# An attention and mixture-of-experts kernel: first-weight splits and block transposes placed along the second products, evictions in program order

## The chip, the cores and the metric

The kernel runs on one core of a Trainium2 chip. The metric is the device time of one execution in microseconds (us). Lower is better. The engines that matter here: TensorE (PE, matrix products; its weight loads are shown as PEld), ScalarE (ACT), VectorE (DVE), GpSimd (POOL, which here mostly issues gathers and scatters) and SyncE (SP, which issues the loads).

## The reference

Attention over 8 batches of 448 tokens with 12 heads of 64, with a soft cap on the scores, then a mixture of 8 experts of which each token goes to one. The second half is what the change touches:

```
scores = cap * tanh(q @ k.T * scale / cap);  attn = softmax(scores) @ v
x      = attn, 3584 tokens of 768
logits = x @ w_gate + modality_bias[modality_id];  e_idx = argmax(logits)
for e in range(8):
    mask = e_idx == e
    h = relu(x[mask] @ w1[e])              # 768 -> 1024
    out[mask] = gate_w[mask] * (h @ w2[e]) # 1024 -> 768
```

## The kernel before, in words

*Blocks.* After the attention the tokens are sorted by expert and done in blocks. In the profiled execution there are eight full blocks of 384 tokens (three tiles of 128), then two blocks of 256 (two tiles), then a rest of at most 32 tokens. Each block has its own expert, or a part of one, and loads that expert's weights.

*Precision.* Every operand of a product is split into a high part (rounded to fp32r) and a low part (what is left), and each product is done three times: high by high, high by low, low by high. Splitting a chunk of weights (`split_w`, lines 952 to 958) is a cast on ACT (line 954) and a subtraction on DVE (line 955). First weights (w1) have six chunks of 128 x 1024, their parts are named ah and al; second weights (w2) have eight chunks of 128 x 768, named bh and bl.

*One block* (`run_slot`, line 1066) runs as follows.
- `load_w2` (line 966) loads and splits the second weights of this block. These are not pinned.
- `ahead` (line 1182) has GpSimd compute an index tile (`index`, line 894) and gather the rows of the next block into `xg` (`gather`, line 928).
- `ffn1` (line 1006) does the first products, lines 1021 to 1025: 8 groups of 18 matmuls, each group into one of three PSUM buffers. ACT evicts a group with a relu (line 1031, hh) and DVE takes the low part (line 1032, hl), after which the buffer is free.
- `load_w1` (line 960) loads and splits the first weights of the next block, and behind its chunks 1 and 3 calls `transpose_all` (line 989): three block transposes of the gathered rows on DVE (line 993), three casts on ACT (line 1002) and three subtractions on DVE (line 1004) for the next block's x.
- `ffn2` (line 1037) does the second products, line 1055: for each tile two halves of 384 columns, 24 matmuls each. In the first tile the halves are interleaved: 21 products of the first half, 9 of the second, the last 3 of the first, and then the rest of the second. A half goes into one of two PSUM buffers (py); when it is done ACT scales it into `ot` (line 1060), and GpSimd scatters the tile to the output (line 1061).

*What sets the order.* Each engine works through one queue in order. The order is laid down before the run by a scheduler that follows program order and estimated readiness, except that an instruction wrapped in `pin` (line 93) stays behind the instruction of its engine that was written before it. `load_w1`, `split_x` within `transpose_all` and the loads are pinned; the eviction of line 1060 is not. Because `load_w1` is written ahead of `ffn2`, all of its instructions have their place in program order ahead of every eviction of `ffn2`.

*Raw buffers.* Loads go to four raw buffers (`load_raw`, line 945) shared by both kinds of weights, in the order first weights of the next block, second weights of the next block, and so on; SP issues a load when the chunk four earlier has been subtracted.

*The last blocks.* The first block of all (`between`) and the rest of few tokens take other ways through `run_slot`; for the blocks of two tiles `load_w2` is written behind `ffn1`.

Of the kernel before, what the change touches and what calls it, by code (L numbers as in the profile page):

```python
# [39 lines left out]
F32 = mybir.dt.float32  # L40
F32R = mybir.dt.float32r
BF16 = mybir.dt.bfloat16
I32 = mybir.dt.int32
# [6 lines left out]
B, H, S, D = 8, 12, 448, 64  # L50
# [11 lines left out]
TW = W // 128  # L62
# [3 lines left out]
KC, FC = DM // 128, FF // 128  # L66
HALF = DM // 2
# [16 lines left out]
class Program:  # L84
# [8 lines left out]
    def pin(self, inst):  # L93
        return self.tc.keep_in_program_order(inst)
# [798 lines left out]

    def index(self, raw, blocks, name="at"):

        at = self.ip.tile([128, 4 * TW], I32, name=name, bufs=2 if name == "at" else 1)
        for t, n in blocks:
            n, w = max(n, 1), 4 * max(n, 1)
            to = at[:, 4 * t : 4 * t + w].rearrange("p (t g) -> p g t", g=4)
            src = raw.bitcast(I32)[:, 4 * t : 4 * t + w, 0].rearrange("p (g t) -> p g t", g=4)  # L900
            self.pin(self.nc.gpsimd.tensor_scalar(to, src, 4.0, self.quarter, op0=ALU.mult, op1=ALU.add))
        return at

    def rows_few(self, meta, row):

        nc = self.nc
        r = self.register(nc.gpsimd, meta[row : row + 1, 1:2], NOROW)
        mt = self.lp.tile([128, 2], F32, name="mf")
        for g in range(4):
            self.pin(nc.gpsimd.dma_start(mt[g * FEW : (g + 1) * FEW], self.mapd[ds(r, FEW)]))  # L910
        index = self.lp.tile([128, 1], I32, name="index")
        self.pin(nc.gpsimd.tensor_scalar(
            index, mt.bitcast(I32)[:, 0:1], 4.0, self.quarter, op0=ALU.mult, op1=ALU.add
        ))
        return mt, index
# [41 lines left out]
            self.pin(a)  # L957
            self.pin(b)

    def load_w1(self, e, spread=True, n=0):  # L960
        for k in range(KC):
            self.split_w(self.load_raw(e, self.w1, k, FF, spread), self.w1s[k], pin=True)
            if n and k in (1, 3):
                self.transpose_all(n, range(3) if k == 1 else range(3, KC))

    def load_w2(self, e, raws=(), ks=range(FC)):
        for k in ks:
# [18 lines left out]
            if pin or t == 0:  # L986
                self.pin(move)

    def transpose_all(self, n, ks=range(KC)):
        turned = [self.lp.tile([128, S], F32, name="turned", tag="xT", bufs=4)[:, : n * 128] for _ in range(3)]  # L990
        for first in ks[::3]:
            for k, out in zip(range(first, first + 3), turned):
                self.pin(self.nc.vector.transpose(
                    out.rearrange("p (c x) -> p c x", x=32),
                    self.xg.bitcast(F32)[:, : 4 * n].rearrange("p c (x k) -> p k c x", k=KC)[:, k],
                ))
            self.split_x(range(first, first + 3), turned, n, pin=self.pin)

    def split_x(self, ks, pts, n=TW, pin=lambda inst: inst):
        w = n * 128  # L1000
# [33 lines left out]
                if at == f:  # L1034
                    work()

    def ffn2(self, mt, n, at={}):

        nc = self.nc
        for t in range(n):  # L1040
            ot = self.lp.tile([128, C * 256], F32, name="ot", tag="late", bufs=3)[:, :DM]
            rows = slice(t * 128, (t + 1) * 128)
            steps = [[(half, f, a, c) for f in range(FC) for a, c in ((0, 0), (0, 1), (1, 0))] for half in range(2)]
            if t == 0:
                late = [(0, f, 0, 1) for f in range(FC - 3, FC)]
                steps = [[step for step in steps[0] if step not in late] + steps[1][:9] + late, steps[1][9:]]
            py, left = [None, None], [3 * FC, 3 * FC]
            for half, f, a, c in steps[0] + steps[1]:
                if a == c == 0 and (2 * t + half, f) in at:
                    at[2 * t + half, f]()  # L1050
                if py[half] is None:
                    py[half] = self.ps_y.tile([128, 512], F32, name="py")
                cs = slice(half * HALF, (half + 1) * HALF)
                left[half] -= 1
                nc.tensor.matmul(  # L1055
                    py[half][:, :HALF], self.h[a][:, f, rows], self.w2s[f][c][:, cs],
                    start=left[half] == 3 * FC - 1, stop=left[half] == 0,
                )
                if left[half] == 0:
                    nc.scalar.mul(ot[:, cs], py[half][:, :HALF], mt[:, t, 1:2])  # L1060
            self.last_out = nc.gpsimd.indirect_dma_start(  # L1061
                self.out, bass.IndirectOffsetOnAxis(ap=mt.bitcast(I32)[:, t, 0:1], axis=0), ot, None,
                bounds_check=NT - 1, oob_is_err=False,
            )

    def run_slot(self, cur, n, ahead=None, between=()):

        at = {}
        if n == TW and not between:
            self.load_w2(cur[0])
        nxt = ahead() if ahead and not between else None
        self.ffn1(n, between)
        if between:
            nxt = ahead()
        if n < TW:
            self.load_w2(cur[0])  # L1080
        if nxt and nxt[2]:
            if between:
                at = {(2, 0): lambda: self.load_w1(nxt[0], False), (4, 4): self.transpose_rows}
            else:
                self.load_w1(nxt[0], n=nxt[2])
        elif nxt:
            e = nxt[0]
            self.load_few(e)
            self.pf = self.ps_h.tile([128, 512], F32, name="ph")
            at = {  # L1090
                (0, FC // 2): self.transpose_few, (1, 0): lambda: self.few1(e, range(4)),
                (2, 0): lambda: self.few1(e, (4, 5)), (2, FC // 2): self.turn_few,
                (3, 0): lambda: self.few2(e, (6, 7, 0, 1)),
            }
        self.ffn2(cur[1], n, at)
        return nxt

    def load_few(self, e):
# [66 lines left out]
    def run_few(self, e, rows):  # L1165

        nc, (mt, index) = self.nc, rows
        self.few2(e, (2, 3, 4, 5), True)
        ot = self.small_tile("of")[:, :QC]
        nc.scalar.mul(ot, self.yf[:, :QC], mt[:, 1:2])  # L1170
        put = nc.gpsimd.indirect_dma_start(  # L1171
            self.out.rearrange("n (g d) -> (n g) d", g=4), bass.IndirectOffsetOnAxis(ap=index[:, 0:1], axis=0), ot, None,
            bounds_check=4 * NT - 1, oob_is_err=False,
        )
        self.tc.declare_no_dep(put.ins, self.last_out.ins, reason="every token is in one slot of the plan")
# [263 lines left out]
```

## Time and profile before

| | us |
|---|---|
| timed runs, lowest / median / highest of 3 | 842.02 / 844.06 / 846.99 |
| the profiled execution, whole | 835.75 |
| its span (first to last instruction) | 834.2 |
| PE busy in the span | 810.5 (97%) |
| PEld busy | 641.3 (77%) |
| DVE busy | 545.8 (65%) |
| ACT busy | 530.4 (64%) |
| POOL busy | 232.6 (28%) |
| granted TensorE clock, mean | 0.996 |

Attention takes up to about 340 us, the blocks the rest. Busy time of PE counts each matmul from its start to its modelled end; neighbours overlap, so a matmul of 0.33 us follows the one before after 0.17 us. An idle time in brackets at the end of a row of the timeline is the time the engine stood still just before, and behind the arrow is what ended it. A wait for several things is put down to the last of them.

### The profile page before, as it was taken

How to read it: one execution, taken by the hardware profiler on the slowest of the kernel's cores; microseconds unless marked ns; L12 is line 12 of the kernel's file. 1: busy time of each engine (PE TensorE's matmuls, PEld its weight loads, DVE VectorE, ACT ScalarE, POOL GpSimd, SP SyncE). 2: the span in 40 equal slices, each digit the busy share in tenths (PEclk: the TensorE clock that was granted, in tenths of full speed). 3: DMA queues.
4: the chain of work that ended last, by engine and by line, in shares of the span. 5: the costliest groups of instructions: out<-in, count | busy, mean ns of one | idle time of the engine just before them, and what ended most of it. 6: DMA issues, size and time to landing. Idle time of an engine off the chain costs nothing. (4 is left out here: it accounts for less than half of the span.)

```text
span 834.2 us, 15255 instructions
## 1 busy us (share of the span) xinstructions
PE 810.5 (97%) x5457; PEld 641.3 (77%) x5457; DVE 545.8 (65%) x1033; ACT 530.4 (64%) x693; POOL 232.6 (28%) x276
## 2 busy tenths in 40 slices
PE   7999999999999999999999999999999999999994
PEld 3445455555545455999999999999999999999993
DVE  7788898989899998956363743637446374447700
ACT  7999999999999998336253542525425254335610
POOL 1000212020202034254417044181441845014100
PEclk9999999999999999999999999999999999999998
DMA  6465564657566645668347373463734647238752
GB/s 205 149 218 176 190 206 169 219 178 229 172 231 164 227 157 156 188 202 297 105 153 245 108 237 105 154 231 114 246 106 150 220 136 236 76 123 273 233 208 100
DMA packets 58555, 152.10 MB, mean 182 GB/s; under 512 B 12203, under 2 KB 22613, under 8 KB 58466
## 3 DMA queue, kind: packets, MB, share of 16 engines
q1 hardware_dynamic: 45200, 117.78, 43.7%
q0 software_dynamic: 13120, 33.22, 11.7%
q8 instruction: 46, 0.75, 0.4%
q14 instruction: 43, 0.35, 0.2%
q10 hardware_dynamic: 146, 0.00, 0.0%
HBM read 114.00 MB, written 22.40 MB: 164 GB/s over the span
## 5 line engine op out<-in xcount | busy, mean ns | idle before, releaser
L542 ACT ACTIVATE th<-sc,isc 128x896 f32<-128x896 f32 x168 | 158.4, 1004 | 3.7 <-PE sc L521 2.2
L1055 PE MATMUL py<-bh,hh 128*128 128x384 f32 x448 | 151.2, 337 | 7.1 <-ACT ot L1060 7.1
L1021 PE MATMUL ph<-x,ah 128*128 128x384 f32 (+1 forms) x480 | 157.2, 328 | 0.5 <-issue 0.5
L1022 PE MATMUL ph<-x,ah 128*128 128x384 f32 (+1 forms) x480 | 156.7, 326 | 0.0
L1025 PE MATMUL ph<-x,al 128*128 128x384 f32 (+1 forms) x480 | 156.6, 326 | 0.0
L1055 PE MATMUL py<-bh,hl 128*128 128x384 f32 x448 | 149.9, 335 | 0.0
L1055 PE MATMUL py<-bl,hh 128*128 128x384 f32 x448 | 146.6, 334 | 0.0
L549 ACT ACTIVATE pt<-th,cabs 128x896 f32<-128x896 f32 x144 | 139.7, 1046 | 0.0
L955 DVE TENSOR_TENSOR bl<-raw,bh 128x768 fp32r<-128x768 f32 x80 | 74.3, 956 | 88.0 <-ACT bh L954 87.2
L1031 ACT ACTIVATE hh<-ph 128x384 fp32r<-128x384 f32 (+1 forms) x80 | 37.5, 469 | 132.4 <-PE ph L1025 127.0
L562 PE MATMUL xT<-pt,va 128*64 128x448 f32 x576 | 118.8, 548 | 0.0
L931 POOL DMA_INDIRECT xg<-xd,at x93 | 101.1, 1087 | 44.1 <-issue 38.4
L1032 DVE SCALAR_TENSOR_TENSOR hl<-ph,hh 128x384 fp32r<-128x384 f32 (+1 forms) x80 | 42.0, 528 | 107.5 <-ACT hh L1031 107.5
L1061 POOL DMA_INDIRECT out_dram<-ot,mt x28 | 30.3, 1082 | 240.7 <-ACT ot L1060 193.1
L1055 PEld LDWEIGHTS py<-bh,hh 128*128 128x128 f32 x448 | 84.1, 188 | 10.8 <-ACT ot L1060 10.1
L1021 PEld LDWEIGHTS ph<-x,ah 128*128 128x128 f32 x480 | 90.1, 188 | 1.6 <-issue 0.9
L1022 PEld LDWEIGHTS ph<-x,ah 128*128 128x128 f32 x480 | 90.1, 188 | 0.0
L1025 PEld LDWEIGHTS ph<-x,al 128*128 128x128 f32 x480 | 90.1, 188 | 0.0
L954 ACT CAST bh<-raw 128x768 fp32r<-128x768 f32 x80 | 64.0, 831 | 32.4 <-DMA raw<-in_w_dram 31.5
L1055 PEld LDWEIGHTS py<-bh,hl 128*128 128x128 f32 x448 | 84.1, 188 | 0.0
L1055 PEld LDWEIGHTS py<-bl,hh 128*128 128x128 f32 x448 | 83.8, 188 | 0.0
L675 POOL DMA_DIRECT2D xd<-xs x24 | 17.0, 709 | 232.9 <-DVE xs L667 226.3
(207 smaller groups left out, 1275.4 us busy)
## 6 DMA issues: line engine op xcount, KB each, us to landing
raw<-in_w_dram SPq DMA_DIRECT2D x86, 384.0 KB, 4.2
raw<-in_w_dram SPq DMA_DIRECT2D x60, 512.0 KB, 5.3
kq<-in_kq_dram SPq DMA_DIRECT2D x47, 448.0 KB, 4.6
va<-in_v_dram SPq DMA_DIRECT2D x24, 448.0 KB, 6.5
xd<-xs POOLq DMA_DIRECT2D x24, 448.0 KB, 5.0
cp<-xT SPq DMA_DIRECT2D x44, 224.0 KB, 2.8
cp<-gl SPq DMA_DIRECT2D x22, 224.0 KB, 2.2
raw<-in_w_dram SPq DMA_DIRECT2D x12, 256.0 KB, 3.8
```

The costliest lines, as they stand in the source:

```text
L542: pin(nc.scalar.activation(th, sc[:, :, :S], AF.Tanh, scale=self.isc))
L549: pin(nc.scalar.activation(e, th, AF.Exp, scale=self.cabs))
L562: pin(pe.matmul(xT[j * D : (j + 1) * D, :S], va[:, u * D : (u + 1) * D], quads[q]["pt"][t, i][:, j], start=t == i == 0, stop=t == 1 and i ...
L931: got = self.nc.gpsimd.indirect_dma_start(self.xg.bitcast(F32)[:, c], None, self.xd.rearrange("n (a x) -> (n a) x", a=4), bass.IndirectOff ...
L954: a = self.nc.scalar.copy(hi, raw)
L955: b = self.nc.vector.tensor_tensor(lo, raw, hi, op=ALU.subtract)
L1021: nc.tensor.matmul(ph[:, :w], hi[:, fs], self.x[k][:, 0, :w], start=first, stop=False)
L1022: nc.tensor.matmul(ph[:, :w], hi[:, fs], self.x[k][:, 1, :w], start=False, stop=False)
L1025: nc.tensor.matmul(ph[:, :w], lo[:, fs], self.x[k][:, 0, :w], start=False, stop=last)
L1031: nc.scalar.activation(hh[:, f, :w], acc, AF.Relu)
L1032: nc.vector.scalar_tensor_tensor(hl[:, f, :w], acc, 0.0, hh[:, f, :w], op0=ALU.max, op1=ALU.subtract)
L1055: nc.tensor.matmul(py[half][:, :HALF], self.h[a][:, f, rows], self.w2s[f][c][:, cs], start=left[half] == 3 * FC - 1, stop=left[half] == 0,)
```

## The change

Five edits:
- `load_w1` takes the chunks to do (`ks`) and no longer calls the transposes.
- `transpose_all` becomes a loop over pairs: `transpose_two` does the two block transposes of a pair at once and returns a function that does the pair's casts and subtractions.
- A new `prepare` makes a table of places in the second products of the running block: chunk k of the next first weights at product step k x halves x 8 / 6 (a half has 8 steps; `halves` is twice the number of tiles), and two steps behind chunks 0 to 3 a turn, which finishes the pair of transposes before and starts the next. For three tiles that is one chunk at the start of each half, and turns at step 2 of halves 0 to 3. `ffn2` calls what stands at a place just before it writes that step's products.
- `ffn2` takes a `pin` for its evictions. It is the real pin where the next block goes through `prepare`, and does nothing elsewhere.
- The two index tiles that are needed late (`at8`, `at9`) come from the pool `lp`, which lies behind the first weights and `xg` in memory, and no longer from `ip`, which lies ahead of them.

```diff
@@ index
-        at = self.ip.tile([128, 4 * TW], I32, name=name, bufs=2 if name == "at" else 1)
+        at = (self.ip if name == "at" else self.lp).tile([128, 4 * TW], I32, name=name)
@@ load_w1
-    def load_w1(self, e, spread=True, n=0):
-        for k in range(KC):
+    def load_w1(self, e, spread=True, ks=range(KC)):
+        for k in ks:
             self.split_w(self.load_raw(e, self.w1, k, FF, spread), self.w1s[k], pin=True)
-            if n and k in (1, 3):
-                self.transpose_all(n, range(3) if k == 1 else range(3, KC))
@@ transpose_all
-    def transpose_all(self, n, ks=range(KC)):
-        turned = [self.lp.tile([128, S], F32, name="turned", tag="xT", bufs=4)[:, : n * 128] for _ in range(3)]
-        for first in ks[::3]:
-            for k, out in zip(range(first, first + 3), turned):
-                self.pin(self.nc.vector.transpose(
-                    out.rearrange("p (c x) -> p c x", x=32),
-                    self.xg.bitcast(F32)[:, : 4 * n].rearrange("p c (x k) -> p k c x", k=KC)[:, k],
-                ))
-            self.split_x(range(first, first + 3), turned, n, pin=self.pin)
+    def transpose_two(self, n, ks):
+        turned = []
+        for k in ks:
+            out = self.lp.tile([128, S], F32, name="turned", tag="xT", bufs=4)[:, : n * 128]
+            self.pin(self.nc.vector.transpose(
+                out.rearrange("p (c x) -> p c x", x=32),
+                self.xg.bitcast(F32)[:, : 4 * n].rearrange("p c (x k) -> p k c x", k=KC)[:, k],
+            ))
+            turned.append(out)
+        return lambda: self.split_x(ks, turned, n, pin=self.pin)
+
+    def transpose_all(self, n):
+        for k in range(0, KC, 2):
+            self.transpose_two(n, (k, k + 1))()
+
+    def prepare(self, e, n, halves):
+
+        split = [lambda: None]
+
+        def turn(k):
+            split.pop()()
+            split.append(self.transpose_two(n, (k, k + 1)) if k < KC else lambda: None)
+
+        at, pos = {}, lambda k, f: divmod(k * halves * FC // KC + f, FC)
+        for k in range(KC):
+            at[pos(k, 0)] = lambda k=k: self.load_w1(e, ks=(k,))
+        for i in range(KC // 2 + 1):
+            at[pos(i, 2)] = lambda i=i: turn(2 * i)
+        return at
@@ ffn2
-    def ffn2(self, mt, n, at={}):
+    def ffn2(self, mt, n, at={}, pin=lambda inst: inst):
...
-                    nc.scalar.mul(ot[:, cs], py[half][:, :HALF], mt[:, t, 1:2])
+                    pin(nc.scalar.mul(ot[:, cs], py[half][:, :HALF], mt[:, t, 1:2]))
@@ run_slot
-                self.load_w1(nxt[0], n=nxt[2])
+                at = self.prepare(nxt[0], nxt[2], 2 * n)
...
-        self.ffn2(cur[1], n, at)
+        self.ffn2(cur[1], n, at, self.pin if nxt and nxt[2] and not between else lambda inst: inst)
```

## Rows read from the trace of the kernel before

**Rows 1.** The page: busy time, share of span and instructions of each engine.
```profile
span 834.2 us, 15255 instructions
PE 810.5 (97%) x5457; PEld 641.3 (77%) x5457; DVE 545.8 (65%) x1033; ACT 530.4 (64%) x693; POOL 232.6 (28%) x276
```

**Rows 2.** Waits: engine and line, what it waited for: us, times, longest.
```profile
...
PEld py L1055 <- ACT ot L1060: 10.1, 9, 1.3
...
PE py L1055 <- ACT ot L1060: 7.1, 8, 1.0
...
```

**Rows 3.** Stretches: length, busy time of PE, PEld, DVE, ACT, POOL, clock, DMA.
```profile
...
411.62:437.82 26.20, 25.28 (x146) 24.96 (x145) 17.72 (x22) 14.78 (x22) 2.16 (x2) 1.00 0.44 137
437.82:463.25 25.43, 25.43 (x145) 25.43 (x145) 8.54 (x13) 7.16 (x12) 16.73 (x19) 1.00 0.62 203
...
782.80:799.61 16.81, 16.81 (x146) 16.81 (x146) 7.95 (x13) 6.82 (x13) 1.11 (x1) 1.00 0.86 311
...
```

**Rows 4.** Timeline of PE: start, us, instruction [idle before]; the first gap.
```profile
...
419.62 0.33 PE L1055 MATMUL py<-bl,hh 128*128 128x384 f32 x1
419.79 0.34 PE L1055 MATMUL py<-bh,hl 128*128 128x384 f32 x1
421.05 0.44 PE L1055 MATMUL py<-bh,hh 128*128 128x384 f32 x1 [0.92 <-ACT ot L1060]
...
```

**Rows 5.** Timeline of PE: the seventh and the eighth gap.
```profile
731.12 0.44 PE L1055 MATMUL py<-bh,hh 128*128 128x384 f32 x1 [0.98 <-ACT ot L1060]
...
778.52 0.44 PE L1055 MATMUL py<-bh,hh 128*128 128x384 f32 x1 [0.35 <-ACT ot L1060]
```

**Rows 6.** Timeline of ACT in the second products that start at 411.62.
```profile
412.20 1.99 ACT L954 CAST ah<-raw 128x1024 fp32r<-128x1024 f32 x2
416.53 0.52 ACT L1002 CAST x<-turned 128x384 fp32r<-128x384 f32 x1 [2.34 <-DVE turned L993]
...
418.52 1.99 ACT L954 CAST ah<-raw 128x1024 fp32r<-128x1024 f32 x2
420.42 1.04 ACT L1060 ACTIVATE ot<-py,mt 128x384 f32<-128x384 f32 x2
...
```

**Rows 7.** Timeline of DVE, the same stretch.
```profile
413.28 2.36 DVE L955 TENSOR_TENSOR al<-raw,ah 128x1024 fp32r<-128x1024 f32 x2 [0.38 <-ACT ah L954]
415.56 2.46 DVE L993 STREAM_TRANSPOSE turned<-xg 128x384 f32<-128x384 f32 x3
...
```

**Rows 8.** Timeline of SP: the fourth and fifth load of second weights.
```profile
...
428.32 0.33 SPq L97 DMA_DIRECT2D raw<-in_w_dram  x1
436.23 2.09 SPq L97 DMA_DIRECT2D raw<-in_w_dram  x3
...
```

**Rows 9.** Timeline of ACT in the first products that start at 437.82.
```profile
...
439.85 0.83 ACT L954 CAST bh<-raw 128x768 fp32r<-128x768 f32 x1 [1.25 <-DMA raw<-in_w_dram]
441.33 0.84 ACT L954 CAST bh<-raw 128x768 fp32r<-128x768 f32 x1 [0.64 <-DMA raw<-in_w_dram]
442.07 0.48 ACT L1031 ACTIVATE hh<-ph 128x384 fp32r<-128x384 f32 x1
...
444.69 0.83 ACT L954 CAST bh<-raw 128x768 fp32r<-128x768 f32 x1 [0.89 <-DMA raw<-in_w_dram]
...
```

**Rows 10.** Timeline of DVE: first low parts of three blocks' first products.
```profile
...
443.07 0.55 DVE L1032 SCALAR_TENSOR_TENSOR hl<-ph,hh 128x384 fp32r<-128x384 f32 x1
...
446.44 0.55 DVE L1032 SCALAR_TENSOR_TENSOR hl<-ph,hh 128x384 fp32r<-128x384 f32 x1
...
703.87 0.55 DVE L1032 SCALAR_TENSOR_TENSOR hl<-ph,hh 128x384 fp32r<-128x384 f32 x1
...
787.82 0.42 DVE L1032 SCALAR_TENSOR_TENSOR hl<-ph,hh 128x256 fp32r<-128x256 f32 x1
...
```

**Rows 11.** Timeline of POOL: the first and last of a block's 12 gathers.
```profile
...
440.51 1.12 POOL L931 DMA_INDIRECT xg<-xd,at  x1 [0.28 <-POOL at L901]
...
455.52 1.00 POOL L931 DMA_INDIRECT xg<-xd,at  x1 [0.31 <-issue]
...
```

## Prediction

> **What bounds the kernel now.** I read the page first: TensorE (PE) is busy 810.5 us of a span of 834.2 us [rows 1], so only gaps on PE are worth anything, and an engine that is busy 65% is not a bound by itself. The view of PE's waits names the gaps: in the products of the experts one kind stands out, a second product (line 1055) that waits for an eviction (line 1060) of ScalarE (ACT): 8 times, 7.1 us in all [rows 2]. The table by stages shows where they sit. One block's second products take 26.20 us with 25.28 us busy; the first products after them take 25.43 us without a gap, 3.18 us for each of the 8 groups [rows 3]. The timeline of PE shows one such gap: matmuls start 0.17 us apart, and then 1.26 us pass from 419.79 to 421.05 [rows 4]. Seven full blocks have one each (0.92 to 0.98 us idle in the row); the eighth, 0.35 us, is in the block of two tiles [rows 4, 5].
>
> What holds it up is seen on ACT. The first half of the first tile has 33 products ahead of its end, so it ends near 411.62 + 33 x 0.173 + 0.33 = 417.7. ACT evicts it only at 420.42: before that it did two weight casts, waited 2.34 us for VectorE (DVE) to have transposed three blocks, cast those, and did two more weight casts up to 420.51 [rows 6]. DVE in turn did both subtractions before the three transposes [rows 7]. Both PSUM buffers of the second products are then full, and the 49th product, due at 419.96, waits for ACT.
>
> **The change part by part.** *Work.* Per block there are still six weight casts, six subtractions, six transposes, six casts and six subtractions of x and six evictions. Durations don't change: a weight cast of 1.05 us, a subtraction of 1.2, a transpose of 0.82, an x cast of 0.52, an eviction of 0.57 [rows 6, 7]. Nothing is added on PE.
>
> *Removed: the stall.* A gap costs PE its idle time and the 0.17 us by which a matmul otherwise overlaps the one before: 1.26 - 0.17 = 1.09 where the row shows 0.92 [rows 4]. Eight gaps: 7.1 + 8 x 0.17 = 8.5 us.
> In the weight-load row the same gaps sum to 10.1 us [rows 2]. The Trainium skill (Perfetto Trace Analysis, Identifying the Most-Contended Engine) says that matmul busy time is a poor measure, since matmuls are pipelined, and takes the busy share of weight loads instead; by that row the sum would be 10.1 rather than 8.5. Starts of matmuls in this trace give 1.09 per gap and not the weight loads' 1.3.
>
> *Does the eviction come in time?* With the new order ACT has ahead of the first eviction two weight casts (to 414.2 [rows 6]) and the first two x casts. DVE subtracts chunk 0 from 413.28 to 414.5 and transposes two blocks to 416.1; the x casts end at 416.7. The eviction can then start at 417.7 and end at 418.3; its buffer is wanted at 419.96. Margin 1.7 us. Every later eviction is due one half (24 x 0.173 = 4.15 us) before its buffer is wanted, and between two of them ACT has at most a weight cast and two x casts, 2.1 us. So all eight gaps should go. That the evictions are pinned costs this: whatever stands behind one on ACT waits for PE to end that half. Those are chunks 2 to 5 of the next first weights, each now a half apart, and through them DVE's subtractions and the loads of SyncE (SP).
>
> *Moved: the loads of the second weights.* They share four raw buffers with the first weights and go out when a chunk has been subtracted. Now the fourth goes at 428.32 and the fifth at 436.23 [rows 8]; the first products begin at 437.82 [rows 3]. Afterwards chunk 5 is cast behind the fifth eviction: five halves from 411.62 end at 432.8 with the tail, eviction to 433.4, cast to 434.4, subtraction to 435.6. First products would begin near 436.7. So the fourth load goes 1.1 us ahead of them instead of 9.5, and the fifth, behind a subtraction of 0.96 us, about at their start instead of 1.6 before. From the fifth's issue to its cast, which waits for its landing, takes 3.6 us [rows 8, 9]; for the fourth this was covered and now isn't. I take the last four splits as 1.6 to 2 us later against the first products. Who waits for them: ACT and DVE have the evictions of the first products in one queue with these splits [rows 9]. Three PSUM buffers hold 9.5 us; the first group's is freed at 443.62, 5.8 us after the start, and the second's at 446.99, 9.2 after, where 12.7 would do [rows 10]. Slack 3.7 and 3.5 us: nothing lost in six blocks. In the last full block (start 437.82 + 5 x 51.68 = 696.2, the stalls being 51.68 apart) the first buffer is freed only at 704.42, slack 1.3 us [rows 10]: 0.3 to 0.7 lost, I take 0.5. In the second block of two tiles (start 782.80 [rows 3], 2.1 us a group, 6.3 us for three) it is freed at 788.24, slack 0.9 us; its loads come 1 to 1.7 us later, so 0 to 0.8, I take 0.5.
>
> *Edits at nothing.* Index tiles behind the weights: the same two small writes, weights and gathered rows at other addresses. The trace has no pair of runs at two addresses; the nearest rows are the gathers, issued 1.3 us apart from 440.51 to 455.52 [rows 11]. The last is issued 7.7 us ahead of the second products that start at 463.25, and the first transpose comes 3.9 us after such a start (415.56 against 411.62 [rows 3, 7]), 2.9 in the new order: 10.6 us cover a slower gather; if that cover went, its excess would show once per block. I take 0, bounds -0.5 and +1 us in all. Pairs instead of threes in the transposes: the same four buffers, 0. The tail, where only the last rows of few tokens run, isn't touched.
>
> *Sum.* 8.5 - 0.5 - 0.5 = 7.5 us. The profiled execution took 835.75 us, 834.2 of it span; it would take 828.25. The timed runs of the same kernel lie at 842.02 to 846.99, median 844.06, about 1% above it. The gain is in gaps of fixed length, so I subtract it: 844.06 - 7.5 = **836.6 us**.
>
> **Rivals.** *Late second weights eat the gain (slower).* The order on ACT and DVE is laid down before the run. If the new one puts the first groups' evictions behind the last split of the second weights, the first buffer is freed only after that. The last split starts 6.9 us after the first products' start now [rows 9]; 2 us later that is 8.9, and with cast 0.83, eviction 0.49, both on DVE another 1.2, it is 11.3 or so where 9.5 is allowed: 1.8 us per block, seven blocks 12.6 us, against 8.5 gained: 848 us. It decides from a first buffer freed 10.7 us after the start (9.5 + 8.5/7). Against it: now two of the last four splits stand ahead of that eviction, and the freeing has 3.7 us. For it: those splits already wait for their loads in the trace [rows 9].
> The Trainium skill (DMA: Bandwidth & Descriptors, Issuing engines are not separate DMA queues) says that transfers of SP and of GpSimd run on the same 16 DMA engines and interleave; by it the delayed loads would meet the gathers, which start 2.7 us into the first products [rows 11], and land later still: 848 would then be a floor. The splits in [rows 9] come 1.6 us apart and wait on DMA, which agrees.
>
> *Half given back.* The same mechanism with the order as it is but 4 us of delay instead of 2: 0.3 to 0.9 us per block, about 4 us: 844.06 - 8.5 + 1 + 4 = 840.5.
>
> *The change doesn't do what it says.* The first eviction now stands fixed behind two x casts, and these behind DVE. If DVE gets to the transposes 2 us later than I count (a late subtraction, a late gather), the gap stays: 844 us. Against it: the 1.7 us margin, and transposes that start 2.3 us behind the first subtraction already, with two subtractions before them [rows 7].
>
> **How the numbers follow.** Forecast 836.6, 0.65; half given back 840.5, 0.14; no effect 844, 0.10; slower 848, 0.11. The forecast's own range is 834 to 839: the sum between 6.5 (both late blocks at their worst, +0.5 for addresses) and 9, and 1.5 us of the median's own spread. For 8 in 10 it must take in the half given back: 833 to 843. Half a per cent, about what a measurement of this kernel tells from no change, is 4.2 us: under 839.8 faster, over 848.3 slower. The forecast lies in faster but for a little (0.63), a part of half given back joins it (0.05): 0.68. Slower takes half of the last rival with its tail: 0.07. Same: 0.25.
>
> **What would show it.** Right: PE's waits on line 1060 gone from the second products; a full block's second products in 25.0 us instead of 26.20; two evictions never back to back on ACT; first eviction starting near 6 us into the second products; weight casts of chunks 2 to 5 each right behind an eviction; the fourth load of second weights near 1 us ahead of the first products. Wrong: PE waiting in lines 1021 to 1025 for line 1032 or 1031 in the fourth or fifth group of a block (the first two rivals, told apart by which splits stand ahead of the first line-1031 eviction), or the gap still at the 49th product (the third). A span off by more than 2 us with all of these right would mean that addresses or something not named here count.

## The result, and the profile after

| | before, us | after, us |
|---|---|---|
| timed runs of the comparison, median (lowest to highest, 4 each) | 845.52 (842.02 to 847.75) | 833.29 (830.53 to 835.14) |
| the profiled execution, whole | 835.75 | 835.14 |
| its span | 834.2 | 833.5 |
| a second comparison: median | 836.59 | 825.26 |
| span of its profiles | 834.2 | 824.9 |

The ratio of the comparison is 0.9856, with a 95% interval of 0.9809 to 0.9903. In the second comparison it is 0.9867 (0.985 to 0.9883), and the kernel before against itself 1.0004 (0.9995 to 1.0014). So the change is worth 1.3 to 1.4%, 11 to 12 us. The forecast was 836.6 us with a range of 833 to 843.

In the first comparison both kernels ran 8 to 9 us longer than in the second, and the profile of after has holds of TensorE there, released by "issue": TensorE stands still for nothing that the profile shows, 5.4 us in all, where its second profile has 0.8. The stretches below are therefore read from the second profile of after.

The page of after, first profile: busy time of each engine, then two groups (line, engine, operation; busy, mean ns; idle time before them and what ended most of it).

```profile
span 833.5 us, 15227 instructions
PE 809.6 (97%) x5457; PEld 639.4 (77%) x5457; DVE 547.3 (66%) x1033; ACT 529.7 (64%) x693; POOL 234.8 (28%) x276
...
L1073 PE MATMUL py<-bh,hh 128*128 128x384 f32 x448 | 150.3, 335 | 0.0
...
L1078 ACT ACTIVATE ot<-py,mt 128x384 f32<-128x384 f32 x56 | 32.6, 583 | 101.6 <-PE py L1073 67.0
```

The work is what it was [rows 1]. The second products (now line 1073) stand idle for nothing, and it is the eviction (now line 1078) that waits for TensorE: who waits for whom has turned round.

Waits of PE in the second profile of after: engine and line, what it waited for: us, times, longest.

```profile
PE sc L528 <- ACT th L542: 3.1, 3, 1.5
PE ph L1039 <- DVE hl L1050: 2.2, 2, 1.8
PE idle L181 <- DVE ones L137: 1.8, 1, 1.8
PE ph L1039 <- issue: 0.8, 1, 0.8
```

The 7.1 us on the eviction [rows 2] are gone. What is new is 2.2 us of a first product that waits for a low part (hl). Both stand beside each other in the table of stretches of the same profile (columns as in [rows 3]): one block's second products and the first products after them, the first products of the last full block, the second products of the first block of two tiles, and the first products of the second (last) one.

```profile
411.27:436.26 24.99, 24.99 (x145) 24.99 (x145) 16.47 (x21) 13.90 (x21) 2.08 (x2) 1.00 0.38 123
436.26:461.22 24.96, 24.96 (x145) 24.96 (x145) 9.75 (x14) 7.67 (x13) 17.20 (x19) 1.00 0.69 227
686.03:710.99 24.96, 24.96 (x145) 24.96 (x145) 9.70 (x14) 7.89 (x13) 8.06 (x7) 1.00 0.58 201
753.93:770.57 16.64, 16.64 (x98) 16.64 (x97) 11.90 (x19) 10.43 (x17) 3.37 (x2) 1.00 0.60 187
770.57:790.49 19.92, 17.69 (x146) 17.16 (x145) 11.22 (x17) 7.76 (x14) 1.42 (x1) 1.00 0.76 273
```

Against [rows 3] three things differ, and only the first was forecast at its size. The second products fell from 26.20 us to 24.99. The first products fell too, from 25.43 to 24.96, though they had no gap to lose: PE was busy throughout in both. And the first products of the last block of two tiles rose from 16.81 to 19.92.

Summed over the starts of PE's matmuls in the second profiles of both kernels, from the first products of the second full block to the end of those of the last block of two tiles:

| stretches | before | after | difference |
|---|---|---|---|
| second products of seven full blocks, to the next block's start | 184.32 | 175.87 | -8.45 |
| first products of seven full blocks | 178.02 | 174.75 | -3.27 |
| first block of two tiles, both products | 34.84 | 33.64 | -1.20 |
| second block of two tiles, first products | 16.80 | 19.92 | +3.12 |
| all of it | | | -9.80 |

The spans differ by 9.3 us, 0.5 less, since the second full block starts 0.6 us later in that profile of after (386.31 against 385.72).

ACT in the second products that start at 411.27 (start, us, instruction, idle before it):

```profile
411.86 1.99 ACT L954 CAST ah<-raw 128x1024 fp32r<-128x1024 f32 x2
415.05 0.52 ACT L1020 CAST x<-turned 128x384 fp32r<-128x384 f32 x1 [1.21 <-DVE turned L991]
415.83 0.51 ACT L1020 CAST x<-turned 128x384 fp32r<-128x384 f32 x1 [0.26 <-DVE turned L991]
417.22 0.58 ACT L1078 ACTIVATE ot<-py,mt 128x384 f32<-128x384 f32 x1 [0.87 <-PE py L1073]
419.82 0.58 ACT L1078 ACTIVATE ot<-py,mt 128x384 f32<-128x384 f32 x1 [2.02 <-PE py L1073]
420.30 1.04 ACT L954 CAST ah<-raw 128x1024 fp32r<-128x1024 f32 x1
...
432.35 0.58 ACT L1078 ACTIVATE ot<-py,mt 128x384 f32<-128x384 f32 x1 [2.69 <-issue]
432.83 1.04 ACT L954 CAST ah<-raw 128x1024 fp32r<-128x1024 f32 x1
```

The first eviction starts 5.95 us into the second products and waits for PE; before, it came at 8.8, two of them back to back, behind seven casts [rows 6]. The casts of chunks 2 to 5 follow an eviction each, the last at 432.83.

### The profile page after: what moved, and what is told of

It reads as the page before. It is cut to its first block, busy times and chain, and to the rows that moved or that the text cites. A ratio compares the mean times of both kernels' runs of the same rounds, so it can differ in the third digit from the quotient of the medians.

```text
span 833.5 us, 15227 instructions
## 1 busy us (share of the span) xinstructions
PE 809.6 (97%) x5457; PEld 639.4 (77%) x5457; DVE 547.3 (66%) x1033; ACT 529.7 (64%) x693; POOL 234.8 (28%) x276
## 5 line engine op out<-in xcount | busy, mean ns | idle before, releaser
L931 POOL DMA_INDIRECT xg<-xd,at x93 | 104.5, 1123 | 46.6 <-issue 38.8
L955 DVE TENSOR_TENSOR al<-raw,ah 128x1024 fp32r<-128x1024 f32 x54 | 65.6, 1220 | 67.2 <-ACT ah L954 60.1
L1078 ACT ACTIVATE ot<-py,mt 128x384 f32<-128x384 f32 x56 | 32.6, 583 | 101.6 <-PE py L1073 67.0
```

The source lines that it names most:

```text
L931: got = self.nc.gpsimd.indirect_dma_start(self.xg.bitcast(F32)[:, c], None, self.xd.rearrange("n (a x) -> (n a) x", a=4), bass.IndirectOff ...
L955: b = self.nc.vector.tensor_tensor(lo, raw, hi, op=ALU.subtract)
```

## Experiments

Three questions were open: which edit brought the part that was not forecast, what held the last small block, and which of the edits are needed at all.

### The two kernels once more

Both kernels unchanged, as the base for the others.

> The kernel before, unchanged, for a second profile. Both theories: ratio 1.000, second products of a full block 26.2 us with one gap at the 49th product. In the profile of the changed kernel PE also stands still in some first products for nothing that the profile shows (rows 'issue', 7 to 8 us in all). If these belong to the chip and the moment, they show here too, 5 to 12 us in all, since the timed runs of the kernel before lie 8 us above its profiled execution. If they come with the change, this profile has none and its span is 834.

> The changed kernel, unchanged. Ratio 0.981 to 0.990. Second products of a full block 25.0 us, first products 24.96 us where no gap falls into them. If the gaps for nothing that the profile shows come with the change, they are in the same blocks as in the first profile; if they belong to the moment, in others.

Measured: 836.59 us, ratio 1.0004 (0.9995 to 1.0014); 825.26 us, ratio 0.9867 (0.985 to 0.9883). What is shown above of the second profiles is from these. The second profile of before has no such holds beyond one of 0.5 us, which by the expectation spoke for the change as their cause; but the second profile of after lacks them too (one of 0.8 us is left), so they are no part of the change.

### The order alone, and the index tiles alone

The order alone is the changed kernel with this line as it was:

```diff
-        at = (self.ip if name == "at" else self.lp).tile([128, 4 * TW], I32, name=name)
+        at = self.ip.tile([128, 4 * TW], I32, name=name, bufs=2 if name == "at" else 1)
```

and the index tiles alone is the kernel before with the same line changed the other way. By the program's allocation that line moves the first weights (ah, al) from byte 66304 of a partition to 66176, and the gathered rows and the pool `lp` with them by the same 128 bytes; x, the second weights and h stay. Every engine's queue is in that kernel what it was before.

> The changed kernel without the move of the index tiles; the order in every engine's queue is that of the changed kernel. Second products 25.0 us in both theories. If addresses set the rate: first products 25.43 us, 2.8 us more than the changed kernel, ratio to before 0.989. If the rate comes from the order: 24.96 and the ratio of the changed kernel.

> The kernel before with only the two index tiles moved behind the weights; the order in every engine's queue is that of the kernel before. If addresses set the rate of the first products: 24.96 us for a full block instead of 25.43 and about 17.1 for one of two tiles instead of 16.9, second products 26.2 as before: 7 x 0.47 - 0.5 = 2.8 us less, ratio 0.997. If the rate comes from the order or from the chip: 25.43 and ratio 1.000.

Measured: order alone 829.4 us, ratio 0.992 (0.9904 to 0.9937); index tiles alone 833.0 us, ratio 0.9959 (0.9946 to 0.9971). Stretches of the order alone: second and first products of a full block, first products of the last small block.

```profile
411.37:436.36 24.99, 24.99 (x146) 24.99 (x145) 16.48 (x21) 13.92 (x21) 2.08 (x2) 1.00 0.36 123
436.36:461.79 25.43, 25.43 (x145) 25.43 (x145) 9.71 (x14) 7.78 (x13) 17.94 (x19) 1.00 0.66 222
773.34:792.92 19.58, 17.35 (x145) 16.94 (x145) 10.73 (x16) 7.76 (x14) 1.68 (x1) 1.00 0.77 279
```

Of the index tiles alone, second and first products of a full block:

```profile
410.92:437.11 26.19, 25.27 (x146) 24.96 (x145) 17.70 (x22) 14.77 (x22) 2.15 (x2) 1.00 0.43 137
437.11:462.07 24.96, 24.96 (x145) 24.96 (x145) 8.54 (x13) 7.16 (x12) 18.09 (x19) 1.00 0.62 206
```

The two parts are separate. The order takes the gaps out of the second products and makes the last small block late; it leaves the first products at 25.43. The index tiles' move leaves the gaps, and the first products fall to 24.96: 144 matmuls at 0.1733 us from start to start on average instead of 0.1766, in every one of the seven blocks. That is 0.47 us a block, 3.3 us in seven. By the ratios, 6.7 and 3.4 us make 10.1 of the 11.1 us that both together brought in the same comparison. The order alone was expected at a ratio of 0.989, which lies outside its interval, although the spans of the two profiles (827.5 and 824.9 us) differ by 2.6 us, near the 2.8 that it was worked out from.

The slow pace is not the same for each matmul. From start to start, slow matmuls of the kernel before repeat 174, 178, 175 and 180 ns, whichever of the three lines they are of, where nearly all of those of the changed kernel lie at 172 to 175.

### What about the place counts

Four kernels with an unread tile in the kernel before and nothing else changed. Three have it ahead of the first weights, of 64, 128 and 256 bytes (16, 32 and 64 columns; here 128):

```diff
+        self.gap = pool("gap", 1).tile([128, 32], F32, name="gap")
+        self.nc.gpsimd.memset(self.gap, 0.0)
```

and one has 128 bytes behind the first weights, so that these stay and only what lies behind them moves: the gathered rows, the pool `lp`, the second weights and h.

> The kernel before with a tile of 128 bytes in each partition that nothing reads, put ahead of the first weights, so that they and all behind them lie 128 bytes higher (in the kernel with the index tiles moved alone they lay 128 bytes lower). No other line is changed. Theory: the place of the operands in SBUF sets the pace of the first products, by its remainder of 256 bytes: full blocks' first products 24.9 to 25.0 us (0.1733 us for each matmul), as with 128 bytes lower, and the two-tile blocks' 17.0 to 17.3; second products unchanged at 26.2; time 832.5 to 834. Rival: it was not the place but the move of the index tiles itself, or the place by another remainder: 25.43 us, 0.1767 us for each matmul, and 835.5 to 837.

> The kernel before with the same unread tile of 128 bytes behind the first weights: these stay where they were, and the gathered rows (xg) and the last pool behind them lie 128 bytes higher. Theory: what counts is where the first weights lie, which TensorE reads; then the first products stay at 25.43 us and the time at 835.5 to 837. Rival: what counts is where the gathered rows or the tiles behind them lie, which are written beside the first products: 24.9 to 25.0 us, 832.5 to 834.

> The kernel before with an unread tile of 64 bytes in each partition ahead of the first weights, which then begin at a remainder of 64 from a multiple of 256 (0 in the kernel before, 128 in the two that ran at 0.1733 us). Theory: any start off a multiple of 256 bytes gives the quicker pace: first products of the full blocks 24.9 to 25.0 us, 832 to 834. Rival: only some remainders do: 25.4 to 25.5 us and 835.5 to 837.

> The kernel before with an unread tile of 256 bytes in each partition ahead of the first weights, which then begin at a multiple of 256 bytes again. Theory: the remainder of 256 counts: 25.4 to 25.5 us for the first products of a full block, as in the kernel before, 835.5 to 837. Rival: the remainder of a larger number counts, or the distance to the other operand: 24.9 to 25.0 us and 832 to 834.

Measured, one run each: 832.82 and 836.93 us beside a kernel before of 836.06; 833.34 and 836.47 beside 837.03. First products of the same full block in the four, in the order above:

```profile
437.11:462.07 24.96, 24.96 (x146) 24.96 (x145) 8.43 (x13) 7.15 (x12) 16.18 (x19) 1.00 0.61 207
```

```profile
437.65:463.10 25.45, 25.45 (x146) 25.45 (x146) 8.46 (x13) 7.14 (x12) 16.78 (x19) 1.00 0.61 203
```

```profile
437.19:462.15 24.96, 24.96 (x145) 24.96 (x145) 8.45 (x13) 7.05 (x12) 16.60 (x19) 1.00 0.63 207
```

```profile
437.11:462.55 25.44, 25.44 (x146) 25.44 (x146) 8.55 (x13) 7.16 (x12) 17.39 (x19) 1.00 0.60 204
```

So it is neither the index tiles themselves nor the gathered rows, but where the first weights lie that TensorE loads. Started at a multiple of 256 bytes (66304, 66560) they give 25.43 to 25.45 us; started 64 or 128 bytes off (66368, 66432, 66176) they give 24.96. Higher or lower is the same. For the first weights other remainders were not tried. The second weights lie off a multiple of 256 in all these kernels by the same allocation (64 bytes in the kernel before, 128 or 192 with 64 or 128 bytes of padding), and the second products run at 0.1733 us in all of them. One rival stays: x, the other operand of the first products, lies at the same place in all these kernels, so the runs can't tell the place of the weights from their distance to x.

### Whether the place fixes the pace

One thing spoke against the place as the whole reason: the first full block's first products run at 0.1733 us in the kernel before, at the same place. This kernel is the kernel before with one matmul more at the head of the first products, which the next one overwrites:

```diff
+            if f == 0 and extra:
+                nc.tensor.matmul(ph[:, :extra], self.w1s[0][0][:, fs], self.x[0][:, 0, :extra], start=True, stop=True)
```

> The kernel before, with the weights where they were, and at the head of the first products of six full blocks one matmul more than needed, whose result the next one overwrites: 32, 64, 128, 192, 256 and 384 columns wide in the second to the seventh of the eight full blocks that the loop runs through; the first and the last have none. Theory: the place of the weights does not fix the pace by itself; TensorE's pipeline falls into one of two paces by how it enters the stretch, so that in some of the six blocks (at least one) the matmuls run at 0.1733 us instead of 0.1767, the block's first products then taking 25.0 to 25.1 us. Rival: with the weights at this place every stretch that follows second products runs at 0.1767 us: 25.45 to 25.7 us in all six.

The blocks with the extra matmul were the third to the eighth full block (the expectation counts them one too low); the widths are 32, 64, 128, 192, 256 and 384 columns in that order. Measured: 835.48 us in one run. The first stretch is the end of the first full block's first products, 71 matmuls; then the blocks with 32, 128 and 192 columns:

```profile
346.95:359.49 12.54, 12.54 (x72) 12.54 (x72) 11.71 (x64) 4.06 (x8) 4.76 (x6) 1.00 0.65 168
437.70:463.25 25.55, 25.55 (x146) 25.55 (x146) 8.50 (x13) 7.17 (x12) 17.96 (x19) 1.00 0.59 203
...
541.28:566.83 25.55, 25.55 (x146) 25.55 (x146) 8.57 (x13) 7.17 (x12) 20.74 (x24) 1.00 0.60 202
593.11:618.19 25.08, 25.08 (x147) 25.08 (x146) 8.55 (x13) 7.16 (x12) 18.09 (x19) 1.00 0.61 204
```

The same 71 matmuls in the second profile of the kernel before:

```profile
346.85:359.18 12.33, 12.33 (x72) 12.33 (x72) 11.73 (x64) 4.07 (x8) 4.52 (x6) 1.00 0.66 144
```

With 192 columns ahead the block ran at the quicker pace, at the slow place: 25.08 us, 0.12 of it the extra matmul as in the others. The other five ran at 25.54 to 25.60. And the first full block, where nothing had been added, ran slowly this time: 12.54 us for 71 matmuls is 0.1766 each, where 12.33 is 0.1737. So there are two paces, each was seen at either place, and a stretch keeps the one that it enters with as long as TensorE isn't held; the place decides which one it is when the stretch follows second products without a pause, in all seven blocks of each kernel here that has no extra matmul and no holds. The first profile of after shows the opposite case, a slow rest of a block at the quick place behind a hold by "issue" at 560.47 (45 matmuls), beside a whole block (144):

```profile
560.75:568.70 7.95, 7.95 (x47) 7.95 (x47) 2.14 (x4) 1.72 (x4) 3.66 (x7) 1.00 0.07 4
593.66:618.63 24.97, 24.97 (x146) 24.97 (x145) 9.97 (x14) 7.90 (x13) 18.69 (x19) 1.00 0.68 226
```

7.95 / 45 is 0.1767, 24.97 / 144 is 0.1734. A hold doesn't always turn the pace: behind those at 408.12 and 509.97 in the same profile it stays at 0.1735 and 0.1734. The first row has DMA at 0.07 and is slow all the same, so DMA traffic isn't what makes the slow pace. What in TensorE keeps it stays open.

The Trainium skill (SBUF — State Buffer, Who interferes with whom) says that TensorE reads its moving operand and its weights through two independent ports and never waits on another engine. The row at 560.75, slow with DMA at 0.07, doesn't speak against this; whether the reads of the two operands get in each other's way, no run here shows. The Trainium skill's formula for the isolated gap between two matmuls (TensorE: Matmul & The Clock Gate, Back-to-back issue gap), columns / 2.4 GHz + 2.5 ns, gives an estimate of 162.5 ns for 384 columns; the traces have 173.3 or 176.7, so the measured pace decides.

### The last small block

In the changed kernel TensorE is held twice in the first products of the last small block, for 1.76 and 0.47 us (timeline of PE, second profile of after):

```profile
781.20 0.39 PE L1039 MATMUL ph<-x,ah 128*128 128x256 f32 x1 [1.76 <-DVE hl L1050]
...
784.05 0.39 PE L1039 MATMUL ph<-x,ah 128*128 128x256 f32 x1 [0.47 <-DVE hl L1050]
```

Followed back on DVE, the lateness begins at a transpose of the few rows (xf) that stands ahead of the last chunk's subtraction and waits for its gather:

```profile
765.81 1.22 DVE L955 TENSOR_TENSOR al<-raw,ah 128x1024 fp32r<-128x1024 f32 x1
770.22 0.54 DVE L1142 STREAM_TRANSPOSE xf<-xg 128x192 f32<-128x192 f32 x1 [3.19 <-DMA xg<-xd,at]
770.68 1.19 DVE L955 TENSOR_TENSOR al<-raw,ah 128x1024 fp32r<-128x1024 f32 x1
```

In the kernel before that transpose stood behind all subtractions and waited for nothing (second profile of before):

```profile
779.46 0.53 DVE L1124 STREAM_TRANSPOSE xf<-xg 128x192 f32<-128x192 f32 x1
```

In a first version it is put in its place by one pin:

```diff
-        nc.vector.transpose(
+        self.pin(nc.vector.transpose(
```

> The changed kernel with one instruction more in the fixed order: the transpose of the few rows (xf, L1142), which in the changed kernel stands in VectorE's queue ahead of the last chunk's subtraction and waited 3.19 us for its gather there. Theory: this wait makes the last low part of the last small block late, and that lateness is the 2.2 us that TensorE waited for hl in that block (first products 19.92 us, 16.80 in the kernel before). Then the first products take 17.2 to 17.8 us, the wait on hl is under 0.6 us, and the ratio is 0.983 to 0.985 where the changed kernel had 0.9867. Rival: the loads of the second weights are late because the first weights are spread over the second products at all; then the transpose makes no difference: 19.4 to 20.0 us, the wait stays at 1.8 to 2.3 us, ratio 0.986 to 0.988.

Measured: 824.71 us, ratio 0.9861 (0.9844 to 0.9877), PE's wait on hl 0.8 us. The first products of the last small block:

```profile
770.21:788.28 18.07, 17.28 (x145) 17.07 (x145) 9.22 (x15) 7.44 (x14) 1.10 (x1) 1.00 0.80 293
```

18.07 us and the wait lie between the two expectations, the ratio in the rival's range. In these profiles the transpose was 1.85 us of the loss, and about 1 us was something else. The first profile of after agrees: there the transpose stood in the same place of the queue but waited for nothing, and the block took 18.53 us.

```profile
775.72 0.56 DVE L1142 STREAM_TRANSPOSE xf<-xg 128x192 f32<-128x192 f32 x1
```

In the timed runs the pin brought 0.5 us, which the intervals don't separate from nothing. The second version adds to it a closer spread in the blocks of two tiles:

```diff
-        at, pos = {}, lambda k, f: divmod(k * halves * FC // KC + f, FC)
+        at, pos = {}, lambda k, f: divmod(k * halves * FC // (KC if halves > 4 else KC + 1) + f, FC)
```

> The changed kernel with the transpose of the few rows (xf) in the fixed order as in the run before, and in the two-tile blocks alone the first-weight chunks spread over six sevenths of the second products instead of all of them (the last chunk stands 12 matmuls, 2.1 us, earlier). Theory: what is left of the loss in the last small block (18.07 us with the transpose moved, 0.8 us of it a wait on hl) is the late end of the spread, which makes the second weights' loads late; then no wait on hl is left, its first products take 17.1 to 17.4 us and the ratio is 0.984 to 0.986. Rival: the loads are late for another reason, their own order in SP's queue or the raw buffers; then 17.9 to 18.5 us and a ratio of 0.986 to 0.987.

Measured: 823.66 us, ratio 0.9847 (0.9831 to 0.9864), no wait on hl.

```profile
770.28:787.39 17.11, 17.11 (x145) 17.11 (x145) 8.59 (x14) 7.55 (x14) 1.10 (x1) 1.00 0.78 287
```

As the theory had it: the stretch gives 0.96 us to the late end of the spread. This is less well shown than the transpose. One profile stands behind it, and in the kernels with the order of before the same block took 16.80 to 18.09 us, the longest (256 bytes of padding) with a wait on hl of 0.8 us. In the timed runs this kernel is the quickest of all (the span of its profile is 821.8 us against 824.9), but the intervals of its ratio and of the changed kernel's still overlap.

### Whether the pairs and the pins are needed

The changed kernel with three transposes behind chunks 1 and 3 again, the chunks spread as in the change:

```diff
+        def chunk(k):
+            self.load_w1(e, ks=(k,))
+            if k in (1, 3):
+                self.transpose_two(n, range(3) if k == 1 else range(3, KC))()
+        return {divmod(k * halves * FC // KC, FC): lambda k=k: chunk(k) for k in range(KC)}
```

> The changed kernel with the block transposes in threes again, behind the second and the fourth chunk, as the kernel before had them; the first weights stay spread over the second products. Theory: spreading the weights alone clears ScalarE's queue, so that the first eviction starts before TensorE wants its bank back (7 us into the second products, wanted at 8.3); then the second products of a full block take 24.9 to 25.1 us, no wait on ot, ratio 0.985 to 0.989. Rival: six splits on ScalarE in a row, three for each half, are still too much beside the casts, and the pairs are needed: TensorE waits on ot for 0.3 us or more in each block, second products 25.3 to 26.2 us, ratio 0.989 to 0.996.

Measured: 826.0 us, ratio 0.9881 (0.9864 to 0.9897). ACT in the second products that start at 410.96:

```profile
416.67 0.52 ACT L1014 CAST x<-turned 128x384 fp32r<-128x384 f32 x1 [0.28 <-DVE turned L991]
417.45 0.51 ACT L1014 CAST x<-turned 128x384 fp32r<-128x384 f32 x1 [0.27 <-DVE turned L991]
417.87 0.58 ACT L1072 ACTIVATE ot<-py,mt 128x384 f32<-128x384 f32 x1
```

The eviction starts 6.9 us in, now behind casts and not behind TensorE, still 1.4 us before TensorE wants the buffer, 8.3 us in. PE waits for no eviction, and full blocks take 24.99 and 24.96 us. So the spread of the chunks alone removes the gaps of full blocks. The pairs may be worth a little elsewhere (the second products of the first block of two tiles take 17.30 us here and 16.64 in the change), which the intervals of the ratios don't separate.

Without the pin on the evictions every engine's queue comes out of the scheduler the same, instruction by instruction, probably because the pinned casts that are written between them hold them in place. So that part of the change does nothing here; no run shows it.

## Why the prediction was right, and where it was wrong

The direction was right, and 833.29 us lies in the range of 833 to 843, near its lower end. It lies 0.7 us under the forecast's own range of 834 to 839, and the drop in that comparison, 12.2 us, is well above the 7.5 of the sum. That the time was in the range is partly luck, as its steps show:

**The gaps: right, a little small.** The eight gaps were taken as 8.5 us. Seven full blocks gave 8.45 us alone, 1.19 to 1.27 in six of them and 1.00 in the last, where 1.09 was reckoned. The missing part is the restart: behind the gap at 421.05 [rows 4] the next matmul starts 0.27 us later and not 0.17 (PE, kernel before):

```profile
421.32 0.34 PE L1055 MATMUL py<-bl,hh 128*128 128x384 f32 x1
```

The first block of two tiles gave 1.2 us more in these two profiles. That makes 9.65, between the 8.5 and the 10.1 of the weight-load row, which the prediction set aside. The order alone was worth 6.7 us in the timed runs: in its profile 9.8 of gaps less 2.8 in the last small block.

**The eviction in time: right.** Start forecast at 6.1 us into the second products (417.7 for 411.62), measured 5.95; full blocks' second products forecast at 25.0, measured 24.99.

**The loads: right in time.** The fourth load of second weights was put 1.1 us ahead of the first products and the fifth near their start. SP, second profile of after, first products from 436.26:

```profile
435.15 0.33 SPq L97 DMA_DIRECT2D raw<-in_w_dram  x1
```

```profile
436.02 1.20 SPq L97 DMA_DIRECT2D raw<-in_w_dram  x2
```

**Their cost: right in six blocks, wrong in the last full one.** DVE's first two low parts of a block, and the first of the last full block (first products from 686.03):

```profile
442.75 0.55 DVE L1050 SCALAR_TENSOR_TENSOR hl<-ph,hh 128x384 fp32r<-128x384 f32 x1
...
446.25 0.54 DVE L1050 SCALAR_TENSOR_TENSOR hl<-ph,hh 128x384 fp32r<-128x384 f32 x1
...
692.29 0.55 DVE L1050 SCALAR_TENSOR_TENSOR hl<-ph,hh 128x384 fp32r<-128x384 f32 x1
```

The first buffer is free 7.0 us after the start instead of 5.8, the second 10.5 instead of 9.2, where 9.5 and 12.7 are allowed [rows 10]. In the last full block it is free after 6.8 us, earlier than before (8.2), and the 0.5 us put down for it was not lost. The rival with the opposite sign, late second weights, was to decide from 10.7 us on; it was 3.7 us short of that.

**The second block of two tiles: mis-sized, 0.5 us against 1.7 to 3.1.** Its first products took 18.53 us in the first profile of after, 19.58 with the order alone and 19.92 in the second profile, against 16.80. The mechanism was the named one, late low parts, and the sign that the prediction gave for it, PE waiting for line 1032 (now 1050) in the fifth group, came in this block alone (781.20). The step that failed is that only the loads were moved in thought. An instruction that isn't written in the changed lines, the transpose of the few rows, has no pin, and the new places of the chunks left it a slot ahead of the last subtraction. In their profiles the two small versions above give back 1.85 and 0.96 us, and with them the block is at 17.11.

**Index tiles at nothing: wrong, the largest miss.** The bounds were -0.5 and +1 us; the edit was worth 3.4 us by itself (ratio 0.9959). The step that failed stands at the prediction's head: only gaps on PE are worth anything. Here TensorE lost time without a gap. The working asked only whether a transfer would be slower at another address and named cover for the gathers. It didn't ask whether the engine that bounds the kernel runs at the same pace at another address, although every matmul of the first products reads a tile that moves. [rows 3] held a hint: in one block 144 matmuls of 384 columns took 25.28 us busy in the second products with their restart, and 25.43 in the first, which had no gap at all. The last sentence of the prediction, that a span off by more than 2 us with everything else right would mean addresses, named the right cause, but the sign itself hardly showed: the sum was 7.5 and the two second profiles differ by 9.3, 1.8 off, because the late block hides most of the gain.

**Pairs at nothing, pins at a price.** The pairs held, in full blocks to 0.1 us. The pins were charged with the late loads of the second weights; as the program is built the queues are the same without them, so the lateness belongs to the new places of the chunks.

The sum by its terms was 8.5 - 0.5 - 0.5 = 7.5; measured 9.65 - 0 - 3.1 + 3.3 = 9.8. Two misses of about 3 us with opposite signs left the forecast close by luck. The time was forecast better than the steps were.

## What to carry over

Where TensorE is the bound, count its matmuls from start to start in every stretch: two stretches of the same shape at 0.1733 and 0.1766 us show a loss that no wait and no gap shows, and moving the weight tiles by 128 bytes was worth 3.4 us here, half of what the edit of the order gave. Where work is moved along a queue, look for the instructions nobody pinned, too: they fall into the new slots, and one that waits for a transfer there holds all behind it.

## What the hardware showed that was not expected

- Two paces of the same matmuls at a granted clock of 1.00: 0.1733 and 0.1766 us for 384 columns. With the first weights at a multiple of 256 bytes all full blocks but the first take the slow one; 64 or 128 bytes off, the quick one. One shorter matmul ahead of a block (192 columns, not 32, 64, 128, 256 or 384) turned slow into quick, and one row of holds turned quick into slow.
- For the blocks of two tiles (256 columns) the places do not agree with this: 16.80 us at the old place and 17.11 at the new one where neither had a wait, so there the new place costs 0.3 us.
- TensorE loses time behind a gap as well (rows at 421.05 and 421.32): the first matmul takes 0.44 us instead of 0.34, and the next starts 0.27 us later and not 0.17.
